# Attention with packed queries and a squared-ReLU MLP: score products in 32x32 PE tiles, the second softmax transposed on VectorE, a new plan

## The chip, the cores and the metric

One core of one Trainium2 chip. A NeuronCore has five engines, each with its own instruction queue: TensorE (PE) multiplies matrices into PSUM, VectorE (DVE) and ScalarE (ACT) read PSUM and SBUF, GpSimd (POOL) and SyncE (SP) mainly issue DMAs here. The metric is the device time of the kernel in microseconds (us), lower is better.

## The reference

Eight batches, 8 heads, 576 tokens of 64 channels; 32 packed queries `p` per head. All float32. Cut to what matters:

```python
def sm_attn(qq, kk, vv):
    s = scale * np.matmul(qq, kk.transpose(0, 1, 3, 2))        # scale = 1 / 8
    a = np.exp(s - np.max(s, axis=-1, keepdims=True))
    a = a / (np.sum(a, axis=-1, keepdims=True) + 1e-09)
    return np.matmul(a, vv)
p_packed = sm_attn(p, k, v)                # (8, 8, 32, 64): 32 packed rows per head
x = sm_attn(q, p_packed, p_packed)         # (8, 8, 576, 64)
x = x.transpose(0, 2, 1, 3).reshape(4608, 512)
out = np.square(np.maximum(x @ w_in, 0.0)) @ w_out             # (512, 2048), (2048, 512)
```

So there are two softmaxes a batch: the first over 576 keys for 32 queries of each head, the second over 32 packed rows for each of 576 tokens of each head.

## The kernel before

Matmul operands are bfloat16, sums float32. Names as in the profile: a line number is that of the kernel file.

**Stages of one batch.** The eight heads are handled as two quartets (`qd`), four heads of 32 rows filling the 128 partitions.

- Loads: `k_b`, `q_b` and `v_b` come through POOL's queue with a cast to bfloat16; `k` of batch 0 comes through SP's queue as float32 into `gT` and is cast on DVE and ACT (L338, L336). `p` comes through ACT's queue (first two batches) and POOL's.
- `tr_k`, `tr_q` (L425, L422): DVE transposes in blocks of 32x32 give `kT`, `qT`, with the channels in 32 partitions of each head and two halves `dh` of the 64 channels beside each other.
- First scores (`s1`, L434 and L436): the packed queries stand in a block-diagonal 128x128 matrix `pT_bd`, so that one full-array matmul serves four heads; each half `dh` is a pass, each pass has 512 and 64 columns.

```python
for dh in range(2):
    nc.tensor.matmul(main, lhsT=w[dh], rhs=kT[:, qd, :GM * P, dh], start=(dh == 0), stop=(dh == 1))
```

- First softmax: maximum on DVE (L440), exponential and sum on ACT (L444), reciprocal and multiplication of all 576 columns on DVE (L450, L451); then five PE transposes a quartet (L457), copied to `e`.
- Value product (`pv`, L472): 40 matmuls of 32 columns in 128x64 tiles. Result `ppT`, channels on partitions.
- `spread` (L484): four matmuls with a permutation `perm`, then four 32-partition copies a batch, make `pq_bd`, block-diagonal for the second scores.
- `m` (L501): the packed rows times `w_in`, in 64x32 tiles, eight matmuls of 512 columns for each of four column chunks of `w_in`. This gives `M` (128 packed rows of a quartet x 2048), so that the MLP's first product is taken over packed rows and not over channels. Even and odd heads use the lower and upper half of the array; a quartet's four results go to the four partition groups of one PSUM bank.
- Second scores (`s2` L522, `s2_rest` L540; batch 0 L533): tokens on the output partitions, `qT` as the stationary operand, 16 matmuls of 128 columns and four in 128x64 tiles for the last 64 tokens.
- Second softmax along the free axis: maximum (L552), subtraction (L557), exponential on ACT (L563), sum and reciprocal (L569, L570), multiplication (L575), all but the exponential on DVE. Nine PE transposes (L584, L586) bring it back to packed rows on partitions, and copies make `a`.
- F1 (`f1_mm` L599, batch 0 in halves of tokens L612): for each of 16 blocks of 128 hidden units, `M` times `a`, four matmuls of 288 columns; ReLU on ACT (L637), square on DVE (L647) into `gT`.
- F2 (`f2_mm` L655, the last tile in two halves L672): for each of 36 tiles of 128 tokens, 16 matmuls of 512 columns of `gT` with `w_out`; copied to `o_sb`, stored through SP's queue, four DMAs a tile.

**What sets the order.** `Plan` is a list scheduler that runs while the kernel is built. Each step has a duration for each engine that can do it, dependencies, PSUM banks that it takes, and a priority out of a table (`TABLE`); what comes out is a fixed order of instructions on each engine. Each engine then runs its queue in order, and waits only on semaphores. Where the plan sees PE idle before the first F2, `keep_clock` (L322) writes matmuls of zeros, 256 columns each, so that PE doesn't idle.

```python
ORDER = ("v0 q0 i0 a0 a1 a2 a3 b0 b1 k1 b2 b3 v1 i1 b4 b5 q1 b6 b7 p2 " ...   # POOL: a: w_in, b: w_out, i: set-up
```

PSUM has eight banks: two pairs of two (`ps`) and four single ones (`pb`). F1, M and the scores take pairs, F2 takes two of the single ones.

Of the kernel before, what the change touches and what calls it, by code (L numbers as in the profile page):

```python
# [23 lines left out]
INF = float("inf")  # L24
HOP = 0.04
LATE = {"PE": 0.17, "ACT": 0.105, "DVE": 0.083}
TURN = 0.098


class Piece:  # L30
    __slots__ = ("step", "stage", "k", "alts", "start", "end", "alt", "prio")

    def __init__(self, step, stage, k, alts):
        self.step, self.stage, self.k, self.alts = step, stage, k, alts


class Step:

    def __init__(self, name, segs, deps=(), take=(), give=(), lag=0.0, banks=(), free=(), mode=0):
        self.name, self.deps, self.take, self.give, self.lag = name, list(deps), list(take), list(give), lag
        n = name.split(".")
        self.key = name if n[1:2] == ["0"] and n[0][0] not in "FL" else ".".join(n[:2])
        self.banks, self.mode = list(banks), mode
        self.free_at = [[t or name for j, t in free if j == i] for i in range(len(segs))]
        self.pieces = [[Piece(self, i, k, p) for k, p in enumerate(st)] for i, st in enumerate(segs)]
        self.give_at = [[(p, t or name) for p, j, t in self.give if j == i] for i in range(len(segs))]


class Plan:

    def __init__(self, slots, nbanks):
        self.nslots, self.nbanks = slots, nbanks
        self.unit = {}
        self.streams, self.base, self.prio, self.lean = [], {}, {}, {}
        self.margin, self.wait, self.levels = 0.0, 0.0, {}  # L60
        self.warm, self.keep = 0.0, None

    def stream(self, steps):
        self.streams.append(list(steps))

    def forward(self):
        slots = {k: [] for k in self.nslots}
        held, done, out, unit = {}, {}, [], {}
        banks = [0.0] * self.nbanks
        busy = dict(self.base)  # L70
        pos = [0] * len(self.streams)
        pend = []
        heap = [0.0]
        seen = -1.0
        mode = 0

        def pick(st, t):
            best, near = None, INF
            for u in st.banks:
                x = max(INF if banks[j] is None else banks[j] for j in u)  # L80
                if x + HOP <= t + 1e-9:
                    return u, t
                near = min(near, x + HOP)
            return None, near

        def ready(st, t):
            r = 0.0
            for d in st.deps:
                x = done.get(d)
                if x is None:  # L90
                    return INF
                r = max(r, x + HOP)
            for p, n in st.take:
                s = slots[p]
                m = len(s) - self.nslots[p]
                for j in range(max(0, m), m + n):
                    if s[j] is None:
                        return INF
                    r = max(r, s[j] + HOP)
            if st.banks:  # L100
                r = max(r, pick(st, t)[1])
            return r

        while heap:
# [4 lines left out]
            while True:  # L109
                cand, soon = [], []  # L110
                for i, steps in enumerate(self.streams):
                    if pos[i] < len(steps):
                        st = steps[pos[i]]
                        r = ready(st, t)
                        if r <= t + 1e-9:
                            cand.append((st.prio, i, st.pieces[0][0], None))
                        elif r < INF:
                            heappush(heap, r)
                            soon.append((st.prio, r, st.pieces[0][0]))
                for x in pend:  # L120
                    if x[1] <= t + 1e-9:
                        cand.append((x[0].step.late, 0, x[0], x))
                    else:
                        heappush(heap, x[1])
                        soon.append((x[0].step.late, x[1], x[0]))
                cand.sort(key=lambda c: c[:2])
                go = None
                for pr, i, pc, x in cand:
                    best = None
                    for a, (e, us, _) in enumerate(pc.alts):  # L130
                        b = t if e == "-" else max(t, busy.get(e, 0.0))
                        v = b + us + (pc.step.lean if e == "ACT" else 0.0)
                        if best is None or v < best[0]:
                            best = (v, b, a, e, us)
                    if best[1] > t + 1e-9:
                        continue
                    e, us = best[3], best[4]
                    if e != "-" and any(p < pr - self.margin and r < t + self.wait and r - t < 0.5 * us and any(z[0] == e for z in q.alts) for p, r, q in soon):
                        continue
                    go = (i, pc, x, best)  # L140
                    break
# [132 lines left out]
def kernel_impl(tc, q, k, v, p, w_in, w_out, out):  # L274
# [15 lines left out]
    with ExitStack() as ctx:  # L290
# [36 lines left out]
        def bank(u, j=0):  # L327
            return half(u[j])
# [655 lines left out]
```

## Time and profile before

| | before |
|---|---|
| time, median of 3 runs | 259.08 us (259.06 to 259.28) |
| span of the profiled execution | 258.9 us |
| PE busy | 247.9 us, 96% |
| DVE busy | 173.9 us, 67% |
| ACT busy | 163.4 us, 63% |
| F2, L655 | x529, 379 ns a matmul, 137.7 us |
| F1, L599 | x448, 286 ns a matmul, 70.7 us |
| clock-keeping matmuls, L322 | x97, 16.3 us |
| granted TensorE clock | 1.00 |

The span runs from the first to the last instruction of one execution; the times of the three runs stand 0.2 to 0.4 above it. Matmuls are pipelined: the duration of one includes the way through the array, and the next starts before it ends, so a sum of durations overlaps itself and a "busy" PE is no proof of a full one. Some matmul records are missing (529 of 560 F2). Starts in the timeline say how long PE was really taken.

### The profile page before, as it was taken

What the parts mean: (1) busy time and instruction counts of PE and PEld (TensorE: products, weight loads), DVE (VectorE), ACT (ScalarE), POOL (GpSimd) and SP (SyncE); (2) the same over time, 40 slices, a digit from 0 to 9 for tenths busy, and PEclk for the clock granted to TensorE, in tenths of its full rate; (3) what the DMA queues carried; (4) which work ended last, traced back from release to release, by engine and by line L of the source; (5) the groups of instructions that cost most, each with busy time, mean ns of one, the idle gap of its engine ahead of it and who ended that gap; (6) DMA issues with size and microseconds to landing.
All of it is one profiled execution on the core that took longest, in us unless ns stands there. A gap on an engine that the chain in (4) does not pass through costs nothing.

```text
span 258.9 us, 5498 instructions
## 1 busy us (share of the span) xinstructions
PE 247.9 (96%) x2154; PEld 146.9 (57%) x2185; DVE 173.9 (67%) x341; ACT 163.4 (63%) x281; POOL 46.5 (18%) x79
## 2 busy tenths in 40 slices
PE   7799999999999999999999999999999999999994
PEld 4477565465644766465665656456563665366452
DVE  3659679998579599956884686927879367546210
ACT  2346988746974758787874844589437784768101
POOL 8646954332424300000000000000000000000000
PEclk9999999999999999999999999999999999999999
DMA  7999999999999994411103111130030211121123
GB/s 219 197 202 207 202 208 197 215 248 227 207 212 231 230 219 96 88 43 44 41 8 86 32 41 43 43 81 22 24 83 7 75 43 28 34 62 41 42 73 90
DMA packets 26617, 29.06 MB, mean 112 GB/s; under 512 B 5472, under 2 KB 18016, under 8 KB 26592
## 3 DMA queue, kind: packets, MB, share of 16 engines
q0 software_dynamic: 18672, 17.96, 42.4%
q1 hardware_dynamic: 7296, 10.56, 14.5%
q8 instruction: 17, 0.28, 0.4%
q10 hardware_dynamic: 624, 0.20, 0.3%
q14 instruction: 8, 0.07, 0.1%
HBM read 37.22 MB, written 9.44 MB: 180 GB/s over the span
## 4 chain that ended last, share of the span: by engine, by line
PE 85%; DVE 6%; ACT 4%; DMA 2%; issue 1%; DVEq 0%; ACTq 0%
PE pb L655 43%; PE ps L599 21%; PE ps L434 3%; PE ps L522 2%; PE ps L612 2%; PE pb L322 2%; PE ps L501 2%; PE pb L472 2%; DMA p_f<-in_p_dram 2%; PE pb L457 2%; PE pb L672 1%; PE pb L501 1%; PE pb L584 1%; ACT gT L628 1%; ACT r L621 1%
## 5 line engine op out<-in xcount | busy, mean ns | idle before, releaser
L655 PE MATMUL pb<-w_out_b,gT 128*128 128x512 bf16 x529 | 137.7, 379 | 1.8 <-issue 0.8
L637 ACT ACTIVATE r<-ps 128x576 bf16<-128x576 f32 x112 | 70.9, 652 | 23.8 <-PE ps L599 20.8
L655 PEld LDWEIGHTS <-gT 128*128 128x128 bf16 x560 | 52.1, 98 | 49.9 <-issue 4.1
L647 DVE TENSOR_TENSOR gT<-r 128x576 bf16<-128x576 bf16 x112 | 49.7, 455 | 33.4 <-ACT r L637 32.5
L599 PE MATMUL ps<-a,M 128*128 128x288 bf16 x448 | 70.7, 286 | 0.5 <-ACT r L637 0.2
L599 PEld LDWEIGHTS <-M 128*128 128x128 bf16 x448 | 43.1, 98 | 22.1 <-issue 2.2
L336 ACT COPY o_sb<-pb 128x512 f32<-128x512 f32 (+1 forms) x19 | 11.0, 577 | 19.7 <-PE pb L655 17.0
L336 ACT CAST M<-ps 128x1024 bf16<-128x1024 f32 (+1 forms) x20 | 17.4, 883 | 8.1 <-PE ps L501 8.1
L338 DVE COPY o_sb<-pb 128x512 f32<-128x512 f32 (+1 forms) x18 | 12.0, 666 | 15.1 <-PE pb L655 8.5
L444 ACT ACTIVATE e1x<-ps,n 128x576 bf16<-128x576 f32 x16 | 11.8, 742 | 15.0 <-DVE n L440 15.0
L322 PE MATMUL pb<-zero 128*128 128x256 bf16 x97 | 16.3, 328 | 1.1 <-DVE zero L341 1.1
L563 ACT ACTIVATE e<-d 128x1152 bf16<-128x1152 f32 (+2 forms) x10 | 9.7, 973 | 11.8 <-DVE d L557 11.6
L440 DVE TENSOR_REDUCE n<-ps 128x1 f32<-128x576 f32 x16 | 11.7, 752 | 5.9 <-PE ps L436 5.8
L336 ACT CAST M<-pb 128x512 bf16<-128x512 f32 x27 | 14.7, 598 | 0.0
L399 POOL DMA_DIRECT2D v_b<-in_v_dram x16 | 11.3, 704 | 14.4 <-DMA k_b<-in_k_dram 9.6
L383 POOL DMA_DIRECT2D q_b<-in_q_dram x16 | 8.9, 562 | 26.5 <-DVE kT L425 16.5
L434 PE MATMUL ps<-kT,pT_bd 128*128 128x512 bf16 x32 | 10.5, 417 | 2.9 <-ACT pT_bd L370 2.2
L322 PEld LDWEIGHTS <-zero 128*128 128x128 bf16 x97 | 10.7, 116 | 4.4 <-DVE zero L341 1.1
L569 DVE TENSOR_REDUCE t<-e 128x36 f32<-128x1152 bf16 (+2 forms) x10 | 11.0, 1099 | 3.2 <-ACT e L563 3.1
L425 DVE STREAM_TRANSPOSE kT<-k_b 128x576 f32<-128x576 f32 x16 | 11.7, 757 | 0.0
L422 DVE STREAM_TRANSPOSE qT<-q_b 128x576 f32<-128x576 f32 x16 | 11.7, 756 | 0.0
L575 DVE TENSOR_TENSOR n<-e,r 128x1152 bf16<-128x1152 bf16 (+2 forms) x10 | 11.1, 1110 | 0.2
(72 smaller groups left out, 236.7 us busy)
## 6 DMA issues: line engine op xcount, KB each, us to landing
out_dram<-o_sb SPq DMA_DIRECT2D x140, 64.0 KB, 1.7
q_b<-in_q_dram POOLq DMA_DIRECT2D x16, 288.0 KB, 11.6
k_b<-in_k_dram POOLq DMA_DIRECT2D x14, 288.0 KB, 12.2
v_b<-in_v_dram POOLq DMA_DIRECT2D x8, 320.0 KB, 11.6
v_b<-in_v_dram POOLq DMA_DIRECT2D x8, 256.0 KB, 11.6
w_in_b<-in_moe_w_in_dram POOLq DMA_DIRECT2D x8, 256.0 KB, 10.5
w_out_b<-in_moe_w_out_dram POOLq DMA_DIRECT2D x8, 256.0 KB, 10.0
gT<-in_k_dram SPq DMA_DIRECT2D x2, 576.0 KB, 5.5
```

Source lines behind the costliest of these rows:

```text
L322: nc.tensor.matmul(half(7)[:, :2 * P], lhsT=zero[:, :P], rhs=zero, start=True, stop=True)
L336: nc.scalar.copy(dst, src)
L338: eng.tensor_copy(dst, src)
L422: nc.vector.transpose(self.qT[:, qd].rearrange("p s x -> p (s x)").bitcast(F32), self.t.q[qd][:].bitcast(F32))
L425: nc.vector.transpose(kT[:, qd].rearrange("p s x -> p (s x)").bitcast(F32).rearrange("p (x a j2) -> p j2 x a", a=32, j2=2), self.t.k[qd][: ...
L434: nc.tensor.matmul(main, lhsT=w[dh], rhs=kT[:, qd, :GM * P, dh], start=(dh == 0), stop=(dh == 1))
L440: nc.vector.tensor_reduce(self.n1[:, qd:qd + 1], self.ps1[qd], axis=AX.X, op=ALU.max, negate=True)
L444: nc.scalar.activation(e1x[:, qd], self.ps1[qd], ACT.Exp, bias=self.n1[:, qd:qd + 1], accum_out=self.d1[:, qd:qd + 1])
L599: nc.tensor.matmul(ps[:, c], lhsT=a.M[:, qd, fb * FB:(fb + 1) * FB], rhs=a.a2[:, qd, c * HALF:(c + 1) * HALF], start=(qd == 0), stop=(qd = ...
L637: nc.scalar.activation(dst, src, ACT.Relu)
L647: eng.tensor_tensor(out=Att.cols(gT[:, fb, o:o + S]), in0=r, in1=r, op=ALU.mult)
L655: nc.tensor.matmul(po[t], lhsT=gT[:, fb, n0:n0 + P], rhs=w_out_b[:, fb, :], start=(fb == 0), stop=(fb == NFB - 1))
```

## The change

The kernel is written anew around the same stages; F1 and F2 are unchanged as products.

- **First scores** (`s1_mm`, new L538): each head's 32 queries are the stationary operand of a 32x32 tile, in the head's own 32 rows. Both quartets go together: head `h` of quartet 0 writes column group `h`, of quartet 1 column group `h ^ 2` (`quad`), so eight tiles are in use. 16 matmuls of 512 and 16 of 64 columns a batch. No `pT_bd`; the factor 1/8 goes into the cast of `p`.
- **First softmax**: no normalisation of the 576 columns; the reciprocals (L566, L568) are multiplied into the 64 channels after the value product (`pp_norm`, L571).
- **Value product** (`pv_mm`, L561): the weights are the stationary operand and `v` moves, 40 matmuls of 64 columns in 128x32 tiles; packed rows on the output partitions. A DVE transpose gives `pq` (L575), one PE transpose and a copy give `ppT` (L578). `perm`, `pq_bd` and their copies go.
- **M** (`m_mm`, L588): in 64x32 tiles as before, with the quartets on the two row halves; rows of `w_in_b` are ordered accordingly, and each of the eight `w_in` pieces is loaded by two DMAs of 64 partitions.
- **Second scores** (`s2_mm`, L604): packed rows on the output partitions, in 32x32 tiles, in two parts of 256 and 320 tokens, 16 matmuls each.
- **Second softmax**: a DVE transpose out of PSUM in 32x32 blocks (`s2_in`, L608), then maximum, subtraction, exponential, sum and multiplication as before in two parts (L611, L620, L623, L626, L627, L631), then a DVE transpose of pairs of bfloat16 (`s2_out`, L637) into `a`. The nine PE transposes and the copies behind them go.
- **PSUM**: three pairs and two single banks, instead of two and four.
- **Loads**: `k` of batch 0 comes first on POOL's queue as all others do; the second `p` load is on SP's queue, float32. `store` writes rows of every second partition.
- **Plan**: a new `Plan` and `TABLE`. A step is now one instruction group; ReLU and square of every batch, M's copies and F2's may go to ACT or DVE.

```diff
-                for dh in range(2):
-                    nc.tensor.matmul(main, lhsT=w[dh], rhs=kT[:, qd, :GM * P, dh], start=(dh == 0), stop=(dh == 1))
...
+            for lo, hi in ((0, GM * P), (GM * P, S)):
+                for x in range(2):
+                    for qd in qds:
+                        for h in range(QH):
+                            c, r = 32 * quad(qd, h), slice(32 * h, 32 * h + 32)
+                            dst = ps1[b, qd][c:c + 32, lo:hi]
...
+                            nc.tensor.matmul(dst, lhsT=pT[r, b * NQD + qd, :, x], rhs=kT[r, qd, lo:hi, x], start=(x == 0), stop=(x == 1))
...
-                nc.vector.tensor_scalar_mul(self.e1n[:, qd], e1x[:, qd], self.r1[:, qd:qd + 1])
...
-                            nc.tensor.matmul(self.ps_pp[64 * e:64 * e + 64, c0:c0 + NP],
-                                             lhsT=self.t.v[:, qd * QH + h, g * D:(g + 1) * D],
-                                             rhs=self.e1[:, qd, g, h * NP:(h + 1) * NP], start=(g == 0), stop=(g == GM))
...
+                        nc.tensor.matmul(t[32 * h:32 * h + 32, qd * D:(qd + 1) * D], lhsT=e1T[:, qd, g, c:c + 32],
+                                         rhs=v_b[b % NV][:, qd * QH + h, g * D:(g + 1) * D], start=(g == 0), stop=(g == GM))
...
-                        nc.tensor.matmul(self.ps_pq[:, x * 64:x * 64 + 64], lhsT=perm[:, x, pr], rhs=self.ppT[:, :, pr],
-                                         start=(pr == 0), stop=(pr == 1))
...
+            nc.vector.transpose(pq[b % 2][:].rearrange("p q i x -> p (q i x)").bitcast(F32), pp[b % 2][:].rearrange("p q d -> p (q d)").bitcast(F32))
...
-                            nc.tensor.matmul(self.ps2[:, tt // 2, c0:c0 + P], lhsT=self.qT[:, qd, tt * P:(tt + 1) * P, dh],
-                                             rhs=self.pq_of(qd, dh), start=(dh == 0), stop=(dh == 1))
...
+            for dh in range(2):
+                for qd in QDS:
+                    for h in range(QH):
+                        c, r = 32 * quad(qd, h), slice(32 * h, 32 * h + 32)
+                        nc.tensor.matmul(t[c:c + 32, qd], lhsT=pq[b % 2][r, qd, :, dh], rhs=qT[r, qd, o:o + w, dh],
+                                         start=(dh == 0), stop=(dh == 1))
...
+            nc.vector.transpose(s2[x][:].rearrange("p q j i -> p q (j i)"), ps2[b, x])
...
-                        nc.tensor.transpose(ps[:, c0:c0 + P], self.n2[:, g0:g0 + QH].rearrange("p g i -> p (g i)"), ident[:])
...
+            for qd in QDS:
+                nc.gpsimd.dma_start(w_in_b[qd * D:(qd + 1) * D, 2 * i:2 * i + 2, c * WCH:(c + 1) * WCH], src[qd][:, 2 * i:2 * i + 2])
...
-        ORDER = ("v0 q0 i0 a0 a1 a2 a3 b0 b1 k1 b2 b3 v1 i1 b4 b5 q1 b6 b7 p2 "
+        ORDER = ("k0 v0 q0 a0 a1 a2 a3 b0 b1 k1 b2 b3 v1 b4 b5 q1 b6 b7 "
```

What the new plan writes on each engine can be counted from the two orders: clock-keeping matmuls (now L468) 137, of which 52 stand ahead of the first scores (before 97 in the profile, 21 ahead); F2 560 and 32 halves in both; DVE ReLUs 43 (before 3), ACT squares 42 (before 12).

1106 lines of the change are left out of this document (471 added, 635 removed), and 199 rows, old and new, of the table TABLE.

## The prediction

> **What bounds the kernel now.** I read the page first, then the timeline of TensorE (PE), then the timelines of VectorE (DVE) and GpSimd (POOL), whose idle notes date the landings. The page, busy time and chain:
>
> ```profile
> span 258.9 us, 5498 instructions
> PE 247.9 (96%) x2154; PEld 146.9 (57%) x2185; DVE 173.9 (67%) x341; ACT 163.4 (63%) x281; POOL 46.5 (18%) x79
> DMA  7999999999999994411103111130030211121123
> PE 85%; DVE 6%; ACT 4%; DMA 2%; issue 1%; DVEq 0%; ACTq 0%
> ```
>
> PE ends the kernel and neither DVE nor ACT is full. DMA is full until slice 15, about 97 us. A busy PE proves little here, so I price its work by starts. First one row of the groups by shape (busy time, mean ns of one), then the timeline of PE (start, busy time):
>
> ```profile
> L501 PE MATMUL ps<-w_in_b,ppT 64*32 64x512 bf16 x136 | 7.0, 386 | 0.2
> ```
>
> ```profile
> 1.07 4.66 PE L322 MATMUL pb<-zero 128*128 128x256 bf16 x21 [1.07 <-DVE zero L341]
> 7.90 1.03 PE L434 MATMUL ps<-kT,pT_bd 128*128 128x512 bf16 x2 [2.17 <-ACT pT_bd L370]
> ...
> 42.05 0.38 PE L655 MATMUL pb<-w_out_b,gT 128*128 128x512 bf16 x1
> 42.36 0.41 PE L501 MATMUL ps<-w_in_b,ppT 64*32 64x512 bf16 x8
> 42.59 0.40 PE L501 MATMUL pb<-w_in_b,ppT 64*32 64x512 bf16 x8
> 42.92 1.25 PE L655 MATMUL pb<-w_out_b,gT 128*128 128x512 bf16 x5
> 44.01 1.06 PE L522 MATMUL ps<-pq_bd,qT 128*128 128x128 bf16 x16
> 44.90 0.38 PE L655 MATMUL pb<-w_out_b,gT 128*128 128x512 bf16 x1
> 45.21 0.30 PE L540 MATMUL pb<-pq_bd,qT 128*64 128x128 bf16 x4
> 45.45 2.76 PE L655 MATMUL pb<-w_out_b,gT 128*128 128x512 bf16 x11
> ...
> 54.18 1.14 PE L599 MATMUL ps<-a,M 128*128 128x288 bf16 x8
> ...
> 59.89 0.61 PE L434 MATMUL ps<-kT,pT_bd 128*128 128x512 bf16 x2
> 60.35 0.22 PE L436 MATMUL ps<-kT,pT_bd 128*128 128x64 bf16 x2
> 60.41 0.38 PE L655 MATMUL pb<-w_out_b,gT 128*128 128x512 bf16 x1
> ```
>
> The reader is to see three things. One: eight tiled matmuls of 512 columns (L501) are over in 0.41 us where one takes 0.386, so they start about 0.003 us apart and run side by side; the next eight start 0.23 later. Two: an excursion into a tiled shape costs about 0.2 beyond its streaming: the F2 before it holds PE 0.31 (42.05 to 42.36) where one F2 takes 0.216 (a run of 29 takes 6.26 in the chain), so 0.09 going in; out, 42.59 to 42.92 is 0.33 for a round of 0.22, so 0.11. Three: from 54.18, the first F1 of batch 1, PE has no room. Up to its end at 255.2 lie 201.0 us. The work written there is 448 F1 matmuls at 0.1225 (four in 0.49), 500 F2 at 0.216, 32 of half width at 0.109, and six batches of attention: 54.9 + 108.0 + 3.5 + 33 = 199.4. The 33 is 5.56 a batch: the 3.71 listed below, 0.56 of e1 transposes, 1.29 for M. Only 1.6 us is waiting. So PE work taken out of this stretch is time taken out, unless the feeding engines fall behind.
>
> **The stretch from 54.18 on, a batch of attention at a time.** Removed or replaced, by starts in the timeline: first scores 2 x 0.52 (59.89 to 60.41) = 1.04; value product 0.74 for forty (L472 in the chain) and 0.09 to enter, 0.83; the spread through `perm` 0.12 (40.63 to 40.75); second scores 0.89 (44.01 to 44.90) and 0.24 + 0.09 for the rest rows, 1.22; the nine PE transposes after the second softmax 0.50 (eight take 0.45, 52.81 to 53.26). Sum 3.71.
>
> Added. First scores: two rounds of eight at 512 columns in one excursion, like L501 from 42.36 to 42.92, 0.56 + 0.09 = 0.65, and two rounds of eight at 64 columns. These cost 0.06 at L501's spacing, or 0.34 at L472's (20 in 0.43, so 0.0215 each); I take 0.06, because eight different tiles follow each other as in L501, where L472 alternates between two. 0.71, bounds 0.65 to 0.99. Second scores: 2 x 256 + 2 x 320 columns are 2.25 rounds of 512, 0.49, and 0.21 for the excursion, 0.70 (0.91 in the one batch where the order puts other work between the halves). Value product: ten rounds of four tiles. L472 gives 20 rounds of two in 0.65 to 0.74, 0.033 to 0.037 a round at 32 columns; at 64 columns a round is between that and twice that, 0.33 to 0.74, middle 0.45, and with 0.2 for the excursion 0.60 to 0.65. One transpose for `ppT` 0.06. Sum 2.1, bounds 1.9 to 2.6. M keeps its four chunks and the order gives it about as many excursions (11 against 12). Saving 1.6 a batch, **9.8 us** over batches 2 to 7 (7 to 11).
>
> The Trainium skill, "TensorE: Matmul & The Clock Gate", part 1 on issue gaps, says that the distance between matmul starts never falls below about 25 ns, however few columns. The L501 rows, 3 ns between tiles, contradict it here; by that rule the 64-column rounds would cost 0.40, and the six batches 2 us more.
>
> **The front, up to the first F1 of batch 1.** Its attention is shorter, but it hangs on loads. The order of loads is kept (batch 0 k, v, q, the eight `w_in` pieces, then `w_out` pieces mixed with batch 1). What changes: k of batch 0 leaves SP's queue and its float32 staging and goes first on POOL's; 4.6 us of memsets and the second `p` load leave POOL's queue, the latter for SP's; each `w_in` piece becomes two DMAs of half the size. POOL always has transfers outstanding, so the bytes decide, and they are the same. I take the landings of before. POOL's timeline dates them: it waits for a landing before it issues the next, so the second q of batch 1 is there at 40.14 and the last `w_out` piece at 42.71.
>
> ```profile
> 40.14 0.56 POOL L383 DMA_DIRECT2D q_b<-in_q_dram  x1 [0.72 <-DMA q_b<-in_q_dram]
> 42.71 0.53 POOL L383 DMA_DIRECT2D k_b<-in_k_dram  x1 [0.70 <-DMA w_out_b<-in_moe_w_out_dram]
> ```
>
> Before, L522 of batch 1 starts at 44.01, four microseconds behind q: `pq_bd` copies (1.19) and `qT` (1.43, from 42.58) are late. After, the copies are gone, so `qT` follows its data: 40.2 + 1.43 + hops, first half of the scores at 41.8. Behind it the new order has 0.44, two F2, the second half 0.49, an M chunk 0.44, then 38 F2 (8.2): F1 of batch 1 at **51.8**, 2.4 earlier. The last piece of `w_out` bounds it too: 38 F2 stand behind it, 42.7 + 8.2 = 50.9. All 64 F2 of tiles 0 to 3 stand ahead of that F1, where before had 60: 4 x 0.216 = 0.9 more done.
>
> One thing pulls the other way. The order writes 52 clock-keeping matmuls (L322, now L468) ahead of the first scores, 21 before. The 21 took 0.222 each, those at 13.31 come every 0.11. So 52 take 5.7 to 11.5, and the first scores start at 6.8 to 12.6, against 7.90; I take 9.6, PE turning fast after some 6 us of unbroken work (4.66 was not enough here, by 13.4 it was fast). The rest of batch 0 in PE's order (85 fillers at 0.11, about 5 of work) then brings its first F1 to about 24 (25.17 before) and, with 26.3 of PE work between, F1 of batch 1 not before 50.3. That is under 51.8: 1.5 us of cover, beyond which each microsecond counts.
>
> **DVE and ACT.** DVE gets two 32x32 transposes from PSUM (512 and 640 columns, 1.5 a batch by the 0.757 of 576 columns) and two of half that (0.95), and loses the 576-column normalisations (2 x 0.375), 6.3 of `pq_bd` copies and most of those to `a2`; max, subtract, sum and multiply stay at about 1.3 each. It also takes 43 ReLUs (3 before), ACT 42 squares (12). Counted by the rows of before, its durations sum to 211 where the same sum gives 185, of which the page counts 173.9 without overlaps; so about 198 of some 247, 80%. Not the bound on average. But in the new order a2 is made just in time: behind the second scores of batch 2 PE has 13.7 us of other work ahead of F1, DVE about 13.5 of work up to the last transpose; batch 4, 11.0 against 10.7; batch 1, 8.7 against 8.5 (DVE by start distances, some 0.085 under the durations). I price half a microsecond at each, **1.5**.
>
> **The sum.** 258.9 - 9.8 - 2.4 - 0.9 + 1.5 = 247.3 us of span. The tail (the last half-width F2 to the last store, 3.7) stays. The three runs of before have a median of 259.08, 0.2 over the profiled span: **247.5**.
>
> **Rivals.** (a) Four row groups do not run side by side. L501 shows two row groups and four column groups; the new scores use four by four, eight tiles at once, all four row groups of a head set writing one PSUM bank. If they take turns by two, each batch costs 1.0 more: 6 + 1 in front, 254.5, still faster. One at a time, each round is four times as long: +3.0 a batch, 18 + 2, **267**, slower; the sign turns at 1.9 a batch. For it: no row shows it. Against: L501's two row groups share a bank in the same round with no loss. The Trainium skill, "TensorEngine Tiling (Array Packing)", Gotcha 1, says that different row tiles cannot use one PSUM bank at the same time. By that rule the L501 rows should be twice as long; they are not, so I give it little. Chance 0.05 for two, 0.04 for one.
>
> (b) The VectorE chain of the second softmax becomes the bound. Place: between second scores and F1 of each batch, and PE's queue behind it. If each of its two dozen DVE instructions costs its full duration instead of its start distance, the chain is 2 us longer, felt in batches 1, 2 and 4: 252. Slower than before needs 1.9 in every batch, the margins of batches 3, 5, 6 and 7 (over 1 us by the order) gone too: 261. Chance 0.05 for the first, 0.10 for the second.
>
> (c) The front gives nothing: the small `w_in` DMAs or the fillers push F1 of batch 1 back to 54. 250.5, chance 0.12.
>
> **Numbers.** The forecast has 0.63, and 0.01 is left for no change. Faster: 0.63 + 0.05 + 0.05 + 0.12 = 0.85; slower 0.14. A difference under 0.2% could not be told from none; the runs of before differ by 0.09%. Range: below, no stall (1.5) nor the 1.6 that PE waits before, F1 of batch 1 at 50.9 (0.9) and the best bound of the attention (1.2) give 242.3; above, (c) and both milder cases, to 254.5. Outside lie the 0.14 slower and some 0.04 below.
>
> **What would show it.** Right: eight score matmuls of 512 columns over in about 0.41 us, then the next eight 0.22 later; first F1 of batch 1 near 51.8; from there to PE's end about 192; PE idle ahead of F1 only in batches 1, 2 and 4. Wrong: score rounds at 0.4 us or more (a); PE waiting on the DVE transposes into `a` in most batches (b); first scores after 11 us or q of batch 1 after 42 (c). A time over 255 means that (a) or (b) holds.

## The result, and the profile after

The changed kernel takes 254.83 us (median of 4 runs, 254.40 to 256.38) where the kernel before, run beside it, takes 259.09 (259.06 to 259.28). The ratio is 0.985, with a 95% interval of 0.982 to 0.988. It is faster, as forecast, but by 4.3 us and not by 11.6: 7.3 above the forecast and 0.3 above the upper end of the range.

The page of the changed kernel, the rows that answer to those of before (span, busy time, chain of waits):

```profile
span 252.3 us, 5981 instructions
PE 237.9 (94%) x2387; PEld 135.8 (54%) x2417; DVE 188.2 (75%) x363; ACT 145.6 (58%) x245; POOL 46.4 (18%) x82
...
PE 51%; DVE 2%; issue 1%; ACT 0%; DVEq 0%
```

PE's busy time fell by 10.0 us, yet its share fell too, from 96% to 94%: PE waits more than before. The chain of waits stops half way here (its shares come to 54%), so I read the timeline of PE instead (start, busy time, and in brackets the idle time ahead and what ended it):

```profile
1.07 7.51 PE L468 MATMUL pb<-zero 128*128 128x256 bf16 x52 [1.07 <-DVE zero L471]
8.51 0.69 PE L538 MATMUL ps<-kT,pT 32*32 32x512 bf16 x16
...
53.64 2.63 PE L647 MATMUL ps<-a,M 128*128 128x288 bf16 x20
57.42 0.39 PE L697 MATMUL pb<-w_out_b,gT 128*128 128x512 bf16 x1 [1.15 <-DVE gT L666]
...
59.15 0.70 PE L538 MATMUL ps<-kT,pT 32*32 32x512 bf16 x32
59.79 0.39 PE L697 MATMUL pb<-w_out_b,gT 128*128 128x512 bf16 x1
...
84.43 0.79 PE L647 MATMUL ps<-a,M 128*128 128x288 bf16 x5 [0.37 <-DVE a L637]
...
106.78 0.70 PE L538 MATMUL ps<-kT,pT 32*32 32x512 bf16 x32 [0.54 <-DVE M L464]
...
187.92 0.23 PE L578 MATMUL ps<-ident,pp 128*128 128x128 bf16 x1 [0.46 <-DVE pp L571]
```

Two things are to be seen. The first scores of a batch, 32 matmuls of which 16 have 512 columns and 16 have 64, hold PE from 59.15 to 59.79: 0.64, where 0.71 was priced; eight of 512 columns start within 0.03, the next eight 0.24 behind them, and the sixteen of 64 all within 0.06. And PE has waits of its own behind 53.64, only one of them (0.37 at 84.43) for `a`, where they were forecast. With 0.29 ahead of L578 at 68.56 and 0.20 ahead of L550 at 109.97 they come to 3.0 us. (Further pauses of 0.16, noted as "issue", lie where records are missing: 2387 matmuls are recorded for 2417 weight loads; a run below with all 2417 has none.)

Set beside the terms of the forecast, with a second profile of the kernel before (the run b_again below):

| | forecast | before, its profile | before, again | after |
|---|---|---|---|---|
| first F1 of batch 1 | 51.8 | 54.18 | 52.74 | 53.64 |
| from there to the end of PE | 191.8 | 201.04 | 200.95 | 193.75 |
| end of PE to end of span | 3.7 | 3.68 | 3.67 | 4.88 |
| time beyond the span | 0.2 | (0.2 assumed) | 1.78 | 2.1 |
| time | 247.5 | 259.1 | 259.14 | 254.4 |

All four terms (the rows above the last) miss by 1.2 to 1.95: 1.85 + 1.95 + 1.2 + 1.9 = 6.9, and the profiled execution of after is 0.4 under its median. The experiments take them one by one.

### The profile page after: what moved, and what is told of

Same layout as the page of the kernel before. It is cut to its first block, busy times and chain, and to the rows that moved or that the text cites. A ratio compares the mean times of both kernels' runs of the same rounds, so it can differ in the third digit from the quotient of the medians.

```text
span 252.3 us, 5981 instructions
## 1 busy us (share of the span) xinstructions
PE 237.9 (94%) x2387; PEld 135.8 (54%) x2417; DVE 188.2 (75%) x363; ACT 145.6 (58%) x245; POOL 46.4 (18%) x82
## 4 chain that ended last, share of the span: by engine, by line
PE 51%; DVE 2%; issue 1%; ACT 0%; DVEq 0%
PE pb L697 30%; PE ps L647 16%; PE ps L588 2%; PE pb L718 1%; PE ps L604 1%; PE ps L550 1%; DVE s L608 1%; DVE qT L518 1%; DVE m L611 1%; PE ps L538 1%; PE ps L561 0%; ACT e1T L462 0%; DVE s L620 0%; PE ps L578 0%; ACT o_sb L462 0%
## 5 line engine op out<-in xcount | busy, mean ns | idle before, releaser
L697 PE MATMUL pb<-w_out_b,gT 128*128 128x512 bf16 x498 | 125.3, 379 | 4.0 <-DVE gT L666 1.1
L656 ACT ACTIVATE r_b<-ps 128x576 bf16<-128x576 f32 x75 | 44.4, 661 | 10.1 <-PE ps L647 8.3
L666 DVE TENSOR_TENSOR gT<-r_b 128x576 bf16<-128x576 bf16 x77 | 33.2, 450 | 14.4 <-ACT r_b L656 12.7
L664 ACT ACTIVATE gT<-r_b 128x576 bf16<-128x576 bf16 x35 | 23.5, 683 | 4.2 <-DVE r_b L658 3.9
L658 DVE TENSOR_SCALAR r_b<-ps 128x576 bf16<-128x576 f32 x37 | 25.5, 749 | 0.1
L544 ACT ACTIVATE e<-ps,n 128x576 bf16<-128x576 f32 x16 | 11.8, 738 | 15.3 <-DVE n L541 15.3
L468 PE MATMUL pb<-zero 128*128 128x256 bf16 x137 | 18.5, 290 | 1.1 <-DVE zero L471 1.1
L468 PEld LDWEIGHTS <-zero 128*128 128x128 bf16 x137 | 13.5, 104 | 4.3 <-DVE zero L471 1.1
L623 ACT ACTIVATE e<-s 128x512 bf16<-128x512 f32 (+1 forms) x16 | 10.7, 684 | 8.5 <-DVE s L620 8.3
L541 DVE TENSOR_REDUCE n<-ps 128x1 f32<-128x576 f32 x16 | 11.6, 738 | 4.8 <-PE ps L538 4.7
L518 DVE STREAM_TRANSPOSE qT<-kq_b 128x576 f32<-128x576 f32 x16 | 11.9, 756 | 2.6 <-DMA kq_b<-in_q_dram 2.5
L521 DVE STREAM_TRANSPOSE kT<-kq_b 128x576 f32<-128x576 f32 x16 | 11.8, 754 | 1.9 <-DMA kq_b<-in_k_dram 1.9
L626 DVE TENSOR_REDUCE t<-e 128x16 f32<-128x512 bf16 (+1 forms) x16 | 11.7, 729 | 2.0 <-ACT e L623 2.0
L608 DVE STREAM_TRANSPOSE s<-ps 128x512 f32<-128x512 f32 (+1 forms) x16 | 12.1, 769 | 0.8 <-PE ps L604 0.5
```

Of the source, the lines that this page charges most:

```text
L468: nc.tensor.matmul(half(7)[:, :2 * P], lhsT=zero[:, :P], rhs=zero, start=True, stop=True)
L518: nc.vector.transpose(qT[:, qd].rearrange("p s x -> p (s x)").bitcast(F32), kq_of["q", b, qd][:].bitcast(F32))
L521: nc.vector.transpose(kT[:, qd].rearrange("p s x -> p (s x)").bitcast(F32).rearrange("p (x a j2) -> p j2 x a", a=32, j2=2), kq_of["k", b, ...
L544: nc.scalar.activation(e1[:, qd], ps1[b, qd], ACT.Exp, bias=n1[b % 2][:, qd:qd + 1], accum_out=d1[b % 2][:, qd:qd + 1])
L608: nc.vector.transpose(s2[x][:].rearrange("p q j i -> p q (j i)"), ps2[b, x])
L656: nc.scalar.activation(dst, src, ACT.Relu)
```

## The experiments

The edits leave the plan and its order as they are unless the text says otherwise, so all other instructions stand where they stood. All ratios are to the kernel before.

### Is 0.2 beyond the span right? (b_again)

The kernel before, unchanged.

> The kernel before, unchanged, to read its own span beside its own time. Theory (the 0.2 around the span was misread): in each execution the time exceeds the span by 1.8 to 2.2 us, as it does in the kernel after, so the usual span of before is about 257.1 and the profiled execution behind the prediction was itself about 1.7 us longer than the usual one. Rival (the new kernel ends worse): before has 0.2 to 0.5 around the span and only the kernel after has 2, so the change itself costs 1.7 there.

Measured: 259.06 us median (258.75 to 259.63), ratio 0.998 [0.997, 1.000]. In ten runs the spans are 256.9 to 257.9 and the time is 1.7 to 1.9 longer each time; the profiled run has 259.14 with a span of 257.4. The theory holds. The profile behind the prediction, span 258.9, was an execution some 1.5 us slower than the usual one. The 0.2 came from setting its span beside the median of other executions. Where the 1.5 lay can be read from the timeline of PE in this profile:

```profile
7.62 0.61 PE L434 MATMUL ps<-kT,pT_bd 128*128 128x512 bf16 x2 [1.96 <-DVE kT L425]
...
8.14 2.46 PE L322 MATMUL pb<-zero 128*128 128x256 bf16 x14
...
52.74 1.02 PE L599 MATMUL ps<-a,M 128*128 128x288 bf16 x7
```

The same fillers in the prediction's profile:

```profile
8.85 3.17 PE L322 MATMUL pb<-zero 128*128 128x256 bf16 x14
```

Two score matmuls take 0.61 here and 1.03 in the prediction's profile, the 14 fillers 2.46 against 3.17, and the first F1 of batch 1 comes at 52.74 against 54.18, although the second q of batch 1 lands at the same time (39.92 and 39.86). So in before the front was set by PE's work of batch 0, and by the time at which PE's matmuls become shorter, which differs from one execution to the next.

### The stores (e1_store, e8_store)

```diff
-   ob[t][64 * i + j2:64 * i + 64:2, o]
+   ob[t][64 * i + 32 * j2:64 * i + 32 * j2 + 32, o]      # e1_store
+   out rows as "(a j) e -> a j e", [:, 2 * jp:2 * jp + 2], from ob[t][64 * i:64 * i + 64, o]   # e8_store
```

> The changed kernel, order of instructions untouched, but each store reads 32 neighbouring partitions of o_sb instead of every second of 64 (so the rows of the output stand in another order; the bytes and the number of DMAs are the same). Theory: the stride over partitions makes each store dearer, 0.59 us of SP against 0.42 and 2.04 us to landing against 1.72, and that is the 1.2 us by which the tail grew. Then issue 0.42, landing 1.7, PE's end to the span's end 3.7 instead of 4.9, PE's end within 0.5 us of 247.4, time about 1.2 lower (253.6). Rival: the tail is longer because the last stores queue up behind each other on SP in the new order; then it stays at 4.9 and the time at 254.8.

> Kernel after, but a store covers 64 neighbouring partitions in one transfer (the two interleaved rows are taken apart on the side of the output in memory), so half as many stores, none with every second partition. Theory (the partition stride of 2 is what made the stores dear): issue 0.42 to 0.45 us, landing 1.7 to 1.8, the stretch after the last matmul 3.3 to 3.7 against 4.88, time 253.1 to 253.5. Rival (the interleaving costs wherever it stands): landing 2.0 or more, stretch after the last matmul 4.3 or more, time above 254.

Measured: e1_store 253.40 us, 0.978 [0.976, 0.980]; e8_store 253.58, 0.977 [0.973, 0.981]. The pages, transfers of stores (count, KB each, median us from issue to landing), of after, e1_store and e8_store in this order:

```profile
out_dram<-o_sb SPq DMA_DIRECT2D x140, 64.0 KB, 2.0
```

```profile
out_dram<-o_sb SPq DMA_DIRECT2D x140, 64.0 KB, 1.7
```

```profile
out_dram<-o_sb SPq DMA_DIRECT2D x70, 128.0 KB, 2.4
```

With neighbouring partitions the same store lands in 1.7 instead of 2.0 and its issue takes 0.42 instead of 0.59 us; the stretch after the last matmul falls from 4.88 to 3.72. Issue, landing and this stretch are as the theory of e1_store has them, to a tenth, and the time is 1.4 lower; only the end of PE is not, at 248.21 and not within 0.5 of 247.4, for in that execution the first F1 of batch 1 came at 54.43 where it came at 53.64 in after. In e8_store two stores become one of twice the size, which lands in 2.4, above the 2.0 that the rival names, though for twice the bytes; the stretch, 3.93, lies between theory and rival, and the time is 0.08 above the theory's range. The new layout of tokens made the tail 1.2 us longer through the stride alone.

### The front: k, p and the pieces of w_in (e3_k0sp, e6_plate, e2_win, e12_piece)

The second q of batch 1 lands at 41.96 to 44.11 in after and its variants that keep the loads, at 39.9 before; so two of these profiles can differ by 2 us here without a change, and after has the earliest. The first F1 of batch 1 follows it by 11.6 to 11.7 (41.96 to 53.64 in after, 43.07 to 54.67 in e8_store, 42.63 to 54.24 in e9_qlate; 12.0 in e4_twice, which has more PE work).

```diff
+   nc.sync.dma_start(stage(qd), k[0, ...])       # e3_k0sp: k of batch 0 on SP's queue, in float32, as before
-   lambda: p_load(1, 2, B, nc.sync)              # e6_plate: second p load on POOL's queue behind the last w_out piece
-   for qd in QDS: ... w_in_b[qd * D:(qd + 1) * D, 2 * i:2 * i + 2, ...]
+   w_in_b[:, 2 * i:2 * i + 2, ...]               # e2_win: one transfer of 128 partitions, 256 KB
+   w_in_b[i * D:(i + 1) * D, :, ...]             # e12_piece: one transfer of 64 partitions, four heads, 256 KB
```

> The changed kernel with the k of batch 0 loaded as before the change: float32 through SP's queue into gT, cast in halves on DVE and ACT right before its transpose; POOL's queue begins with v. The order of all else is untouched. Theory: the front is late because POOL's first transfers start later than SP's did, and the queue carries that lateness to q of batch 1. Then the second q of batch 1 lands at 40.2 to 40.9 (POOL's wait for it ended at 42.24), the first F1 of batch 1 starts near 52 (53.64), the 1.43 us hole of PE at 56 shrinks by as much, time 1.5 to 3 us lower. Rival: the w_in pieces in two DMAs each make the lateness; then q of batch 1 moves by less than 0.5 us and the time by less than 0.7.

> Kernel after, but the second p load (384 KB) is issued on the GpSimd queue behind the last w_out piece, where before had it, not on SP's at the start; its cast and transpose move from 32.5 to the k of batch 2 in VectorE's order. Theory (the 384 KB ahead of batch 0 make all later loads late): the second q of batch 0 lands at 12.9 (13.92), the last w_in at 24.6 (25.68), the second q of batch 1 at 40.9 (41.96), first F1 of batch 1 at 52.6 (53.64); VectorE's wait for q of batch 2 near 53 stays, since the bytes then stand ahead of it; time 253.8. Rival (the small w_in transfers alone make them late, or the front is not set by loads): q of batch 1 within 0.3 of 41.96, first F1 of batch 1 within 0.3 of 53.64, time 254.5 to 255.

> Kernel after, but each w_in piece is again one transfer over 128 partitions instead of two over 64; the rows of w_in lie in another order than the heads of M want them, same bytes and same work. Theory (splitting the pieces costs transfer time): the last w_in piece lands 0.9 us earlier (24.8 against 25.68), the second q of batch 1 at 41.1 (41.96), first F1 of batch 1 near 52.8 (53.64), time 254.0. Rival (only the bytes ahead count, the second p load among them): landings within 0.2 of those of after, time within 0.3 of it (254.6).

> Kernel after, with w_in cut otherwise: each transfer has all four heads of one half of the partitions (64 partitions, 256 KB), eight transfers as before the change, where after has sixteen of 128 KB. Theory (a queue holds eight transfers, so smaller ones leave fewer bytes under way and the memory idles between 20 and 23 us): last w_in at 24.8, second q of batch 1 near 41.1, time 253.1 to 253.7. Rival (64 partitions at a time are slow whatever their size): landings within 0.3 of those of after (25.7 to 26.4 and 42 to 43), time 254.6 to 255.2.

| | time | ratio | last w_in | second q of batch 1 | first F1 of batch 1 |
|---|---|---|---|---|---|
| after | 254.83 | 0.985 [0.982, 0.988] | 25.68 | 41.96 | 53.64 |
| e3_k0sp | 255.16 | 0.986 [0.983, 0.988] | 26.70 | 42.98 | 54.66 |
| e6_plate | 255.72 | 0.986 [0.981, 0.990] | 25.31 | 42.68 | 54.38 |
| e2_win | 253.08 | 0.974 [0.971, 0.978] | 24.81 | 41.09 | 53.09 |
| e12_piece | 252.85 | 0.975 [0.974, 0.977] | 24.91 | 41.19 | 52.95 |

Neither k on its old queue nor the late p load makes the front earlier; both profiles lie within the spread of unchanged loads, so the theories of e3_k0sp and e6_plate fall, and the bounds of their rivals were too narrow. Sixteen transfers of 128 KB instead of eight of 256 KB do matter, and 64 partitions as such do not: e12_piece keeps them and is as fast as e2_win. The landings of both are as their theories have them; the times are 0.9 and 0.25 lower than they say. More profiles say the same: q of batch 1 lands at 41.96 or later in all nine that cut `w_in` as after does, and at 40.93 to 41.65 in the six with pieces of 256 KB (best4, best5, best7 and best8, below, among them). (e2_win's output is not the reference's, since its rows of `w_in` stand in another order; e12_piece keeps the order.) The windows of 20 to 24 us (busy time of each engine, then granted clock, DMA share, GB/s) show where, first after, then e12_piece:

```profile
20.00:24.00 4.00, 4.00 (x40) 2.95 (x38) 3.76 (x8) 2.64 (x5) 4.00 (x8) 1.00 1.15 166
```

```profile
20.00:24.00 4.00, 4.00 (x47) 2.94 (x47) 3.93 (x9) 2.92 (x6) 2.67 (x6) 1.00 1.24 206
```

The issues and landings in after show that POOL issues a transfer when the eighth before it has landed (the one at 14.21 behind the landing at 13.92), so eight at most are under way: 1 MB with small pieces, 2 MB with large ones. That alone is not the dip. From 14 to 20 us after carries 200 GB/s with 0.9 to 1 MB under way, as e12_piece does with 2 MB (202); the dip, 117 GB/s from 21 to 22, comes with seven or eight transfers under way, and its lowest point, at 21.4, ahead of the 1.96 us that POOL then spends on memsets (from 21.65). Small pieces also cost POOL more time of its own: 0.59 us an issue at 128 KB, 0.61 at 256 KB, so that POOL is busy for all of the 8 us from 20 to 28 in after and for 4.92 in e12_piece. No run separates these two; what is shown is that the cut makes the dip. All nine profiles with small pieces fall to 117 GB/s or less in some microsecond between 20 and 24, and none of the six with large ones falls under 194. The Trainium skill, "DMA: Bandwidth & Descriptors", Rules for kernel authors, advises one transfer of 128 partitions in place of two to the two halves, because both halves spread over the same engines; the trace agrees that two halves bring nothing, but puts the price on their size: halves of 256 KB cost nothing (24.91 against 24.81 for the last piece).

### Is PE the bound, and is VectorE? (e4_twice, e5_nomax)

```diff
-   for dh in range(2):
+   for dh in (0, 1, 0, 1):     # e4_twice: second scores twice
...
    def s2_max(b, x):
+       return                  # e5_nomax: and s2_sub: no maximum, no subtraction
```

> The changed kernel with every second-score product made twice into the same PSUM region (same result, order of all else untouched): 32 more tiled matmuls a batch, 2.25 rounds of eight at 512 columns, 0.49 us of PE. Theory: from the first F1 of batch 1 on PE is the bound, so six batches cost 6 x 0.49 = 3.0 us, and up to 0.5 more in front: time 257.3 to 258.4. Rival: VectorE's queue has become the bound; then PE has room and the time rises by less than 1.0.

> The changed kernel without the maximum and its subtraction in the second softmax (32 DVE instructions less, 2.7 us of DVE a batch; the exponential reads the transposed scores; same value in exact arithmetic as the scores are small). Order of all else untouched. Theory: PE is the bound, so only the waits ahead of F1 come back, 1 to 2 us: time 252.8 to 253.8, and PE's work from the first F1 of batch 1 to its end takes 191 to 193 instead of 193.75. Rival: VectorE is the bound; then at least 5 us come back, up to 16.

Measured: e4_twice 258.66 us, 0.999 [0.997, 1.002], 3.8 slower than after, 0.3 above the theory's range; e5_nomax 254.59, 0.981 [0.978, 0.985], no gain that stands clear of after, which neither theory nor rival had. That 3.8 is near eight times 0.49 is chance. In the profile of e4_twice, 4.2 longer than that of after, the stretch from the first F1 of batch 1 to PE's end is 195.44, only 1.7 longer: PE's work in it grew by 3.0 as priced (without the noted waits 193.8 against 190.7), but its waits fell from 3.0 to 1.7. The rest, 2.5, stands in front, where q of batch 1 landed at 44.11, and 0.5 of PE work in batch 0 doesn't explain that. So PE work counts there less what waits take up, and VectorE's load does not count: with 2.7 us of it a batch taken away the stretch is 194.06. But the profile of e5_nomax holds a clue. PE's wait near 107 has not gone with VectorE's work, it has grown to 1.75, and this is what ScalarE and VectorE do ahead of it (timelines of ACT, then DVE):

```profile
102.41 0.59 ACT L462 COPY o_sb<-pb 128x512 f32<-128x512 f32 x1 [2.38 <-DMA out_dram<-o_sb]
102.89 1.26 ACT L623 ACTIVATE e<-s 128x512 bf16<-128x512 f32 x2
```

```profile
103.56 0.69 DVE L626 TENSOR_REDUCE t<-e 128x16 f32<-128x512 bf16 x1 [4.15 <-ACT e L623]
```

VectorE waits 4.15 us for the exponentials, these stand in ScalarE's queue behind the copy of an output tile, and that copy waits 2.38 for a store.

### Do the waits only move? (e9_qlate)

The largest wait of PE in after, 1.15 at 57.42, is for a square on VectorE. Ahead of the squares VectorE's queue has the transposes of q of batch 2, and the second of these waits for its transfer, which lands at 55.19 (VectorE's rows of after):

```profile
55.22 0.78 DVE L518 STREAM_TRANSPOSE qT<-kq_b 128x576 f32<-128x576 f32 x1 [1.19 <-DMA kq_b<-in_q_dram]
...
56.58 1.15 DVE L666 TENSOR_TENSOR gT<-r_b 128x576 bf16<-128x576 bf16 x3
```

```diff
    def f1_sq(b, fb, eng):
+       if b == 1 and fb in (5, 7):
+           tr_q(2, (5, 7).index(fb), True)     # instead of ahead of all squares of batch 1
```

> Kernel after, with the two transposes of q of batch 2 moved in VectorE's order from ahead of all squares of batch 1 to behind the first five of them, so that the squares no longer queue behind a transfer. Theory (that order turns the lateness of the loads into PE's largest wait, 1.15 us at 57.42): the wait is gone, first F1 of batch 1 to PE's end falls from 193.75 to 192.6, time 253.4 to 254.0. Rival (the wait only moves to the next place where VectorE is late, as taking the maximum away did): a wait of 1 us or more appears near 106.8, the stretch stays within 0.3 of 193.75, time 254.4 to 255.

Measured: 255.36 us, 0.985 [0.983, 0.988], the stretch 193.90: the rival, with a time 0.4 above its range. The wait at 57 is gone, and PE waits near 107 instead:

```profile
107.54 0.65 PE L540 MATMUL ps<-kT,pT 32*32 32x512 bf16 x17 [1.16 <-DVE M L464]
```

### The output buffers (e11_rot)

The plan gives a tile the first of four output buffers that it thinks free, 2.5 us after a store. In the loaded stretch a store takes up to 6.9 us to land. The waits of ScalarE for stores (us in all, times, longest) and the rows around the one near 102 in after:

```profile
ACT o_sb L462 <- DMA out_dram<-o_sb: 6.2, 4, 2.3
```

```profile
102.20 0.59 ACT L462 COPY o_sb<-pb 128x512 f32<-128x512 f32 x1 [1.16 <-DMA out_dram<-o_sb]
102.68 1.26 ACT L623 ACTIVATE e<-s 128x512 bf16<-128x512 f32 x2
```

```profile
103.35 0.69 DVE L626 TENSOR_REDUCE t<-e 128x16 f32<-128x512 bf16 x1 [0.87 <-ACT e L623]
...
104.24 1.38 DVE L521 STREAM_TRANSPOSE kT<-kq_b 128x576 f32<-128x576 f32 x2
105.55 1.18 DVE L464 CAST M<-ps 128x1024 bf16<-128x1024 f32 x1
```

Store, copy, exponential, sum, transposes of k, copy of M, first scores: seven steps in four queues, and PE's 0.54 at 106.78 is the end of them.

```diff
-   ob[t] = o_sb[u[0] - 14]
+   ob[t] = o_sb[t % NO]
```

> Kernel after, with the four output buffers taken in turn instead of the first that the plan thinks free. Theory (the plan reuses a buffer 2.5 us after its store, while a store in the loaded stretch takes up to 6.9 us to land, so ScalarE waits for it, in the kernel after 6.2 us in four waits, and the exponentials and with them VectorE and the first scores of batch 4 are late): ScalarE's waits for stores are gone or under 1 us, the wait of PE near 106.8 falls from 0.54 to under 0.2, stretch from the first F1 of batch 1 to PE's end 193.75 to 193.2, time 254.1 to 254.6. Rival (these waits lie beside other work): the wait near 106.8 stays at 0.4 to 0.6 and the time within 0.3 of 254.8.

Measured: 252.76 us, 0.975 [0.973, 0.976]: 2.1 less than after, where I had expected some 0.5. ScalarE has no wait for a store left, and of PE's waits from the first F1 of batch 1 on one of 0.46 (L578) is left. The stretch falls from 193.75 to 191.14. Part of that is the wait at 57.42: in this profile the first F1 came late (55.06), so q of batch 2 (55.64) held it up less; that part is not the buffers'. Where after waits at 106.78, PE goes straight on:

```profile
104.93 1.24 PE L697 MATMUL pb<-w_out_b,gT 128*128 128x512 bf16 x5
106.10 0.70 PE L538 MATMUL ps<-kT,pT 32*32 32x512 bf16 x32
```

### Together (best2, best1, best3, best4, best5, best7, best8)

A first attempt cut w_in by single heads over all partitions, with the stores of e8_store; best1 has the late p load besides, best3 the later transposes of q.

```diff
+   for h in (2 * i, 2 * i + 1):
+       nc.gpsimd.dma_start(w_in_b[:, h, c * WCH:(c + 1) * WCH], src[h])    # src: "(qd h d) f -> h qd d f"
```

> Kernel after with the two costs taken away that two runs showed by themselves: stores over 64 neighbouring partitions, and each w_in piece as two transfers of one head over all 128 partitions instead of two heads over 64. As many w_in transfers as after, so it also tells what made the pieces slow. Theory (half the partitions made them slow): as with one transfer a piece, last w_in at 24.8, second q of batch 1 near 41.1; with the stores' 1.2, time 251.7 to 252.3. Rival (the number of transfers made them slow): q of batch 1 at 42 to 43, time 253.2 to 253.7, as with the stores alone.

> As the run best2, and the second p load behind the last w_out piece on the GpSimd queue. Theory (with the pieces whole, the 384 KB ahead of batch 0 are what is left of the lateness): second q of batch 1 0.7 earlier than in best2, time 0.5 lower. Rival (the p load costs the same wherever it stands, as moving it alone showed): time within 0.4 of best2, or up to 0.5 above it, for q of batch 2 behind it comes later and VectorE waits for that.

> As the run best2, and the transposes of q of batch 2 behind the first five squares of batch 1. Theory: where the loads are earlier the wait at 57 is already short, so it brings 0.3 or less over best2. Rival (the wait stays at 1 us): 0.8 to 1.1 less than best2.

Measured: 262.03 (1.011 [1.009, 1.013]), 262.47 and 263.02 us. Both theories missed: the last w_in piece lands at 33.96. The pages of e8_store, which has the same stores, and of best2 say how:

```profile
DMA packets 25563, 28.70 MB, mean 114 GB/s; under 512 B 4416, under 2 KB 16960, under 8 KB 25536
```

```profile
DMA packets 39899, 28.76 MB, mean 111 GB/s; under 512 B 18752, under 2 KB 31296, under 8 KB 39872
```

The sixteen transfers of one head were cut into 14,336 more packets under 512 bytes, 896 for each 128 KB. Why this form and not the others is cut so is open; with so large a loss these three runs say nothing on p and q.

The next ones take w_in as in e12_piece, the stores of e8_store and the buffers of e11_rot (best4); best5 adds the later transposes of q, best7 the late p load, best8 two more output buffers.

> Kernel after with three repairs at once: stores over 64 neighbouring partitions, w_in in eight transfers of 256 KB, the output buffers in turn. If each has its own place, the gains add: 1.2 for the stores, 1.4 for w_in, 0.4 for the buffers, 251.6 to 252.2. Rival (w_in by 64 partitions gives nothing): 253.0 to 253.5.

> As the run best4, and the transposes of q of batch 2 behind the first five squares of batch 1. Theory (the two waits stand one behind the other: with ScalarE's wait for stores gone, the one for q no longer comes back near 106.8): 0.6 to 1.1 less than best4. Rival (with w_in earlier there is no wait for q left to remove): within 0.3 of best4.

> As the run best4, and the second p load behind the last w_out piece on the GpSimd queue. Theory (with w_in at full depth the 384 KB ahead of batch 0 are the rest of the lateness, 41.17 for the second q of batch 1 against the 40.2 predicted): that q near 40.4, first F1 of batch 1 near 52.0 against 52.76, time 249.5 to 249.9. Rival (the load costs the same wherever it stands, VectorE then waits for q of batch 2 or for p): 250.2 to 251.

> As the run best4, with six output buffers in turn instead of four. Theory (one wait of ScalarE for a store is left, 2.9 us, and lies beside other work): time within 0.3 of best4, 250.1 to 250.6. Rival (it still delays PE): 249.6 or less.

| | time | ratio | first F1 of batch 1 | to the end of PE | to the end of span |
|---|---|---|---|---|---|
| best4 | 250.36 | 0.966 [0.964, 0.967] | 52.76 | 191.33 | 3.99 |
| best5 | 250.98 | 0.968 [0.967, 0.969] | 53.23 | 191.87 | 3.97 |
| best7 | 252.17 | 0.974 [0.971, 0.977] | 52.97 | 192.51 | 4.05 |
| best8 | 250.12 | 0.965 [0.964, 0.966] | 53.28 | 191.26 | 3.94 |

The page of best4:

```profile
span 248.1 us, 5890 instructions
...
PE 89%; DVE 5%; ACT 3%; issue 1%; DVEq 0%; ACTq 0%
```

The three repairs came to 2.0 + 1.3 + 2.1 = 5.3 us one at a time and give 4.5 together, more than the 2.6 to 3.2 expected. PE is on 89% of the chain again and its one wait behind the first F1 of batch 1 is the 0.46 ahead of L578. Moving q's transposes costs 0.6 (the theory of best5 falls, and its rival too): there was no wait left to remove. In the profiles, 1.0 apart, 0.5 lies in front of the first F1 of batch 1, ahead of what was moved, for a reason that no run shows. The late p load costs 1.8, more than even its rival had: q of batch 2 lands at 54.63 instead of 53.52 behind it, and PE's wait at 57 is back with 1.25. In e6_plate that wait is 1.65, but e1_store, which leaves the load where it is, has 1.78, so there it proves nothing. The two further buffers bring nothing (the intervals of best8 and best4 overlap); the two waits for a store that best4 has left, 2.9 of ScalarE and 9.1 of VectorE, lie beside other work. best4 and best8 are the fastest versions, 8.9 and 9.0 us under the kernel before as it ran beside them (259.26 and 259.11).

## Why the prediction was right and wrong

The direction was right, and so was the cause of the gain; four terms of the sum were not, and all four erred the same way.

**Right: PE is the bound, and the attention was priced well.** From the first F1 of batch 1 on, e4_twice lengthens PE's work by the 3.0 that were added, and e5_nomax, with less work on VectorE, gains nothing. The stretch before holds 200.95 us, of which 0.3 are noted as waits; after, 193.75 with 3.0. So 9.9 us of PE's time went, where 9.8 + 0.9 = 10.7 was written: without the 0.9 for the F2 done ahead, 1.5 a batch, against 1.6 (six times 1.6 is 9.6, not the 9.8 written).

**Right: rival (a) has nothing to it.** Four row groups of 32 run side by side into one bank: sixteen matmuls of 512 columns, 0.388 each, and sixteen of 64 are over in 0.64. The Trainium skill, "TensorEngine Tiling (Array Packing)", Gotcha 1, says that they cannot; this row contradicts it too. Rival (b) falls with the waits for `a`, 0.37 in one batch and not in most, and with e5_nomax: VectorE's work could be cut without any gain.

**Wrong: the front, 1.85 us.** The step that failed is "POOL always has transfers outstanding, so the bytes decide, and they are the same". How the bytes are cut decides too: sixteen pieces instead of eight bring a dip near 21 us, and the last of them lands at 25.68 instead of 24.91. With large pieces the q of batch 1 lands at 40.9 to 41.7, not at 40.2, and the first F1 comes at 52.8 to 53.3. So the pieces account for 0.7 of the 1.85 in the profiles of after and e12_piece, and for more in the other profiles with small ones; the last microsecond is open (k and p, the two loads ahead that were moved, were put back one at a time, and neither is its cause by itself). From q on, the working held: 51.8 - 40.2 = 11.6, and 11.7 was measured (11.6 to 12.0 over all versions). The fillers were not late: the first scores start at 8.51, before the 9.6 taken. Set against b_again the front is 0.9 later, not 2.4 earlier, so the place that rival (c) names came true for the most part (53.64 against 54), in part through the small `w_in` transfers that it names: 0.12 was too little for it. Its price of 250.5 doesn't follow from its own terms, which give 247.5 + 2.2 = 249.7. The lead of 2.4 was also read against a front that was slow in that one execution (54.18 where 52.74 is usual).

**Wrong: the stalls, 1.95 with the 0.8 short of work.** The term "a2 is made just in time", 1.5, measured 0.37, in batch 2 alone. But the waits rose by 2.7, and most are waits that no step had: 1.15 for a load that stands in VectorE's queue ahead of squares, and 0.54 and 0.20 (at 106.78 and 109.97) for output buffers through ScalarE's queue, both gone in e11_rot. The 0.46 ahead of L578 in the last batch stays in best4 and best8, and for the 0.29 at 68.56 no cause was sought. The prediction followed the order of PE and VectorE; the plan's choice of buffers, and what it believes of a store, was in neither.

**Wrong: the tail, 1.2.** That it "stays" was taken from the instructions' names and number. Their pattern had changed: every second partition.

**Wrong: 0.2 around the span, 1.9.** It is 1.7 to 2.2 in every execution of either kernel. The 0.2 compared the span of one execution with the times of others. A profile's span and the time must come from the same run.

With the three repairs best4 has a span of 248.1 where the forecast was 247.3. That is near in part by luck: its front is 1.0 later than forecast and its tail 0.3 longer, and its stretch is 0.5 shorter only because 0.46 of waits are left where 1.5 were forecast.

## What to carry to other kernels

When a change re-cuts loads or rearranges rows, price each transfer again, by its size, by the number of issues, and by its pattern on the side of the chip: equal bytes are not equal time. When a plan picks buffers, look up after which delay it thinks them free and compare it with the landings in the busiest stretch. And when a wait that you removed comes back elsewhere, follow the queues backwards from there: here a store, two engines away, held PE. And where work is added to find the bound, read the stretch it was added to: the time alone agreed with the price by chance.

## What the runs showed of the hardware

- Stores from every second partition: issue 0.59 against 0.42 us, landing 2.0 against 1.7 for the same 64 KB.
- With at most eight transfers of POOL's queue under way, pieces of 128 KB and of 256 KB both carried 200 to 202 GB/s from 14 to 20 us; from 20 to 24 the kernel with small pieces carried 166 and the one with large pieces 206. One issue took POOL 0.59 and 0.61.
- A load of 128 partitions with one run of 512 elements each, from rows in two blocks of 64, was cut into small packets (16,267 for 2.29 MB from 13 to 34 us, 141 bytes each on average), and the last of sixteen landed 8.3 us later than with the same bytes two heads at a time.
- PE's first score matmuls of the kernel before took 1.03 us a pair in one execution and 0.61 in another, and the first F1 of batch 1 moved by 1.4 us with it. The granted clock does not show it: its first two slices are 9 and 9 tenths in the slow one, 9 and 7 in the fast one.
